# A sparse-attention and PReLU feed-forward kernel: batch 0 reordered over all engines, casts and copies in halves, layer 1 of chunk 0 woven into its end

## The chip, the cores and the metric

The kernel runs on 1 core of one Trainium2 chip. The metric is the device time of one execution in microseconds (us). The engines are TensorE (PE, with its weight loads shown as PEld), VectorE (DVE), ScalarE (ACT), GpSimd (POOL) and SyncE (SP, which here only issues DMAs). Each engine takes its own instructions in order and waits on semaphores for the others. Matmul results go to PSUM, everything else lives in SBUF.

## The reference

```python
q, k, v: (8, 8, 576, 64)            # batch, heads, positions, head size
scores = q @ k^T / 8
mask, heads 0-3: 0 <= i - j < 32                     # local
mask, heads 4-7: i >= j and i % 32 == j % 32         # strided
attn = softmax(masked scores) @ v
x = attn.transpose(0, 2, 1, 3).reshape(4608, 512)    # 8 * 576 tokens
h = x @ w_in                                         # 512 -> 2048
g = max(h, 0) + alpha * min(h, 0)
out = g @ w_out                                      # 2048 -> 512
```

Inputs and output are float32.

## The kernel before

**Units of work.** Attention is cut into 32 pairs of heads, four to a batch; pair g belongs to batch g // 4. Of the four pairs of a batch, 0 and 1 are local and 2 and 3 strided. The feed-forward part is cut into 9 chunks of 512 tokens. Layer 1 of a chunk is 16 blocks m of four 128x128 by 512 matmuls (`lin1_piece`, L652), each followed by ACT (`neg`, L662) and DVE (`gT`, L665). Layer 2 of chunks 0 and 1 is 16 pieces of four matmuls (`lin2_piece`, L679), four to one block of 128 output rows, which ACT copies out (L684) and SP stores (L685). From chunk 2 on layer 2 uses seven products of a Strassen-like scheme (`lin2_sums`, L771), with sums of weights in `wsum` and, in place in `wout16`, `w3` (`w_sums`, L711).

**Attention of a pair.** `transpose_piece` (T) turns q or k with eight PE transposes into a PSUM tile `tp`, which is copied to `qT` or `kT`; `tails` does the last 64 positions. For batches 0 and 1 the copy of `tp` is split by head `e`, one half on DVE and one on ACT (lines L190 and L188 of the helper `cast_copy`; L192 is its POOL form). `score_piece` (S) computes half of a pair's scores and, for batch 0, adds the mask by a matmul (L377) ahead of the exponential on ACT (L382, L385). `pv_piece` (P) multiplies by V with a column of ones and divides on DVE: a reciprocal (L478) and a product (L480). `x_piece` (X) transposes the result back, and a copy puts it into `xT`, layer 1's input. Batches 0 and 1 take this way (`NEARLY = 2`); from batch 2 on the strided q and k are turned by DMA transposes on SP (`transpose_d`, L137) and the masks are multiplied on POOL (L436, L443).

**PSUM.** Eight banks: a pool of three for `tp`, `tt`, `pv` and `xp` (tag "ps"), two for `sp`, and three (`banks`, picked in turn by `hbank`) for layers 1 and 2. In batch 0 two of these three serve scores and the third takes filler matmuls on zeros (`warm`, L829).

**Loads.** POOL issues nearly all of them, in this order at the start: tails, q and k of the local heads, V, the four quarters of `w_in` (`win`), of `w_out` (`wout`), then all of batch 1. Between the issues POOL does casts: local q and k (`cast_l`), half of V (`cast_v`), and `over_v`, which copies a part of the local V tile to other partitions. SP issues the strided k, the constants and later the stores and DMA transposes.

**Order.** The function `alone` writes out the order of batches 0 and 1 by hand into the list `pieces`. All of batch 0 runs before any layer 1:

```python
fns = [T(u0, "q"), T(u0, "k"), Sc(A[0], 0), Sc(A[0], 1), T(u1, "q"), Sc(A[1], 0), T(u1, "k")]
fns += [Sc(A[1], 1), Sc(L[0], 0), Pv(A[0], 0), Sc(L[0], 1), Pv(A[0], 1), Pv(A[0], 2)]
```

Here u0 is the strided unit, u1 the local one, A and L their pairs. Then layer 1 of chunk 0 runs alone, 16 blocks; then layer 2 of chunk 0, with the 22 pieces of batch 1 spread between its 16 pieces by a list of counts, and after them the two transposes of batch 2's local heads. From chunk 1 on, attention of batch n + 1 is spread evenly between the blocks of chunk n. Chunk 1's layer 1 needs batch 1, as 448 of its tokens lie in it.

Of the kernel before, what the change touches and what calls it, by code (L numbers as in the profile page):

```python
# [31 lines left out]
def kernel(  # L32
# [112 lines left out]
                cast_copy(eng[f], t16[:, f : f + 1, :], loaded[(b, True, nm)][:, f : f + 1, :])  # L145
        cast16[(b, True, nm)] = t16

    def cast_l(b, nm, eng="pool"):
        t16 = hpool.tile([128, 8, 2, 64], F16, tag=f"{nm}l16", bufs=2, name=f"{nm}l16")
        cast_copy(eng, t16, loaded[(b, False, nm)].rearrange("p f (t d) -> p t f d", t=8))  # L150
        cast16[(b, False, nm)] = t16

    def load_tail(b, strided):

# [44 lines left out]
                      "p (h t d) -> p h t d", h=2, t=8))  # L199
        cast16[(b, True, "v")] = v16  # L200

    def over_v(b, eng):

        v16 = vls[b % 2]
        cast_copy(eng, v16[0:32, 1:24, :], v16[96:128, 0:23, :])


    class Pair:
# [25 lines left out]
    def transpose_piece(u, nm):  # L234

        b, strided = u // 2, u % 2 == 1  # L240
        early = b < NEARLY
        src = cast16[(b, strided, nm)]
        dst = qTs[u % 2][:, :, 0:576] if nm == "q" else kTs[u % 2][:, :, 32:608]
        if early and nm == "k":
            tails(b, u, strided)
        tp = pspool.tile([128, 8, 64, 2], F16, tag="ps", name="tp")
        for j in range(8):
            blk = (src[:, j % 2, 128 * (j // 2) : 128 * (j // 2) + 128] if strided
                   else src[:, j].rearrange("p f d -> p (f d)"))
            keep(nc.tensor.transpose(tp[:, j].rearrange("r p e -> r (p e)"), blk, ident))  # L250
        if strided:
            main = tp.rearrange("r j p e -> r e j p")
            o = dst.rearrange("r e (j p) -> r e j p", j=8)[:, :, :, 0:64]
        else:
            main = tp.rearrange("r t p e -> r e p t")
            o = dst[:, :, 0:512].rearrange("r e (p t) -> r e p t", t=8)
        if early:
            for e in range(2):
                eng = "dve" if (nm == "q") == (e == 0) else "act"
                if u == 0 and nm == "q":  # L260
                    eng = "dve"
                cast_copy(eng, o[:, e : e + 1], main[:, e : e + 1])
            return
        cast_copy("act", o, main)
        if nm == "k":
            tails(b, u, strided)

    def tails(b, u, strided):
# [216 lines left out]
    def x_piece(P):  # L485
        xp = pspool.tile([128, 1024], F16, tag="ps", name="xp")
        for t in range(P.n):
            keep(nc.tensor.transpose(  # L488
                xp[:, P.w * t : P.w * t + P.w], P.x16[0 : P.w, 128 * t : 128 * t + 128], ident[0 : P.w, 0 : P.w]))
        base = (P.b % 4) * S  # L490
        if P.strided:
            keep(nc.scalar.copy(
                xT[:, P.hp, base : base + S].rearrange("r (p t) -> r p t", t=8),
                xp[:, 0:576].rearrange("r (t p) -> r p t", t=8)))
        else:
            cast_copy("act" if P.b < NEARLY and P.hp == 0 else "dve",
                      xT[:, P.hp, base : base + S], xp[:, 0:576])

    def x_dma(P):
# [21 lines left out]
    def T(u, nm):  # L521
        return lambda: transpose_piece(u, nm)
# [10 lines left out]
    def alone(u0, u1):  # L533

        A, L = (2 * u0, 2 * u0 + 1), (2 * u1, 2 * u1 + 1)

        def Sb(g):
            return lambda: score_early(pairs[g])

        if u0 == 1:  # L540
            fns = [T(u0, "q"), T(u0, "k"), Sc(A[0], 0), Sc(A[0], 1), T(u1, "q"), Sc(A[1], 0), T(u1, "k")]
            fns += [Sc(A[1], 1), Sc(L[0], 0), Pv(A[0], 0), Sc(L[0], 1), Pv(A[0], 1), Pv(A[0], 2)]
            fns += [Sc(L[1], 0), Pv(A[1], 0), Sc(L[1], 1), Pv(A[1], 1), Pv(A[1], 2)]
        else:
            fns = [T(u0, "q"), T(u0, "k"), Sb(A[0]), Sb(A[1])]
            fns += [Pv(A[0], 0), T(u1, "q"), Pv(A[0], 1), T(u1, "k"), Pv(A[0], 2), Sb(L[0])]
            fns += [Pv(A[1], 0), Pv(A[1], 1), Sb(L[1]), Pv(A[1], 2)]
        fns += [Pv(L[0], 0), X(A[0]), Pv(L[0], 1), X(A[1])]
        fns += [Pv(L[1], 0), Pv(L[1], 1), X(L[0]), X(L[1])]
        for fn in fns:  # L550
            feed(fn, -1)

    alone(1, 0)
    end0 = len(pieces)
    alone(3, 2)
    end1 = len(pieces)

# [81 lines left out]

    gTs = {}  # L640

    def lin1_piece(n, m):
        if m == 0:
            gTs[n] = gpool.tile([128, 16, 512], F16, tag="gT", name="gT")
        c0 = (512 * n) % RING
        parts = [(c0, 0, min(512, RING - c0))]
        if c0 + 512 > RING:
            parts.append((0, RING - c0, 512 - (RING - c0)))
        hps = hbank()
        for kk in range(4):  # L650
            for x, (src, dst, w) in enumerate(parts):
                keep(nc.tensor.matmul(  # L652
                    hps[:, dst : dst + w],
                    win16[:, kk, 128 * m : 128 * m + 128],
                    xT[:, kk, src : src + w],
                    start=(kk == 0 and x == 0),
                    stop=(kk == 3 and x == len(parts) - 1),
                    skip_group_check=True,
                ))

        neg = npool.tile([128, 512], F32, tag="neg", name="neg")
        keep(nc.scalar.activation(neg, hps, AF.Relu, scale=-1.0))  # L662

        def fin():
            keep(nc.vector.scalar_tensor_tensor(  # L665
                gTs[n][:, m, :], neg, oma[:, m : m + 1], hps, op0=ALU.mult, op1=ALU.add))
        late.append(fin)
# [28 lines left out]

        return wout16[:, 8 * i : 8 * i + 8, 256 * j : 256 * j + 256]

    def w_sums(eng, which):

        w1, w2, w4 = wsum
        w3 = wq(0, 1)
        steps = {
            1: (w1, wq(0, 1), wq(0, 0), ALU.subtract),
            2: (w2, wq(1, 1), w1, ALU.subtract),
            3: (w3, wq(1, 1), wq(0, 1), ALU.subtract),
            4: (w4, wq(1, 0), w2, ALU.subtract),
        }
        for z in which:
            o, x, y, op = steps[z]  # L710
            keep(eng.tensor_tensor(o, x, y, op=op))  # L711

    def g_sum(eng, n, which, k0, k1):

# [153 lines left out]
    load_v(0, True)  # L868
    load_v(0, False)
    load_w(0, False)  # L870
    cast_l(0, "q")
    load_w(1, False)
    cast_l(0, "k")
    load_w(2, False)
    load_w(3, False)
    cast_v(0, 1, "pool")
    over_v(0, "pool")
    for c in range(4):
        load_w(c, True)
    load_unit(1, True)  # L880
    load_unit(1, False)

    warm(12)
    keep(nc.vector.tensor_copy(id16, ident[0:16, 0:16]))
    cast_s(0, "q", ("dve", "act"))
    cast_s(0, "k", ("dve", "act"))
    keep(nc.vector.tensor_scalar(
        madd, consts[:, 128:488], -1.0, 30000.0, op0=ALU.add, op1=ALU.mult))
    apt = pspool.tile([128, 512], F32, tag="ps", name="apt")
    for i in range(end0):  # L890
        if i == 3:
            keep(nc.tensor.transpose(apt[:, 0:16], alpha_r, id16))
            keep(nc.vector.tensor_scalar(
                oma, apt[:, 0:16], -1.0, 1.0, op0=ALU.mult, op1=ALU.add))
        if i == 8:
            cast_v(0, 0, "dve")
        attn_step(end0)
        if i < 2:
            warm(4 - i)
        elif i > 8 and i not in (10, 13, 15):  # L900
            warm(1)

    def attn_n(n, end):
        for _ in range(n):
# [16 lines left out]
    cast_l(2, "k")  # L921


    turn.append(2)
    for m in range(16):
        lin1_piece(0, m)
        attn_n(0, end1)
    for i in range(16):
        lin2_piece(0, i)
        attn_n((0, 1, 1, 1, 1, 2, 1, 2, 1, 2, 1, 2, 2, 3, 2, 0)[i], end1)  # L930
        if i > 13:
            attn_n(1, end1 + 2)
    assert pos["i"] == end1 + 2
    wide["on"] = False
    load_unit(3, False)
# [2 lines left out]
    for n in range(1, NCH):  # L938
        ab = attn_until(n + 1) if n + 1 < B else len(pieces)
        left = ab - pos["i"]  # L940
        acc = 0.0
        for i in range(32 if n == 1 else 30):
            second["on"] = i >= 16
            if i < 16:
                if n > 1:
                    lin1_piece(n, {13: 7, 14: 14}.get(i, 8 * (i % 2) + i // 2))
                    if i in (5, 9, 13):
                        g_sum(nc.gpsimd, n, 1, i // 2 - 2, i // 2)
                else:
                    lin1_piece(n, i)  # L950
            elif n == 1:
                lin2_piece(n, i - 16)
                if i in (18, 22, 26):
                    w_sums(nc.vector, ({18: 1, 22: 2, 26: 4}[i],))
            else:
                lin2_sums(n, i - 16)
                if n == 2 and i == 20:
                    w_sums(nc.vector, (3,))
            if n < B - 2 or i < 16 or i > 19:
                acc += left / (22.5 if n == 1 else 16 if n == B - 2 else 20.5) * (0.5 if i < 16 else 1.0)  # L960
            cnt = int(acc)
            acc -= cnt
            attn_n(cnt, ab)
        while pos["i"] < ab:
            attn_step(ab)
# [30 lines left out]
```

The softmax here doesn't subtract the row's maximum and nothing guards it: scores larger than these inputs give would overflow.

## Time and profile before

| What | Value |
|---|---|
| median of 6 runs | 305.31 us (305.21 to 305.67) |
| the profiled execution, its own time | 305.27 us |
| its span (first to last instruction) | 303.5 us |
| PE busy | 294.7 us, 97% of the span |
| DVE, ACT, POOL busy | 221.2, 177.6, 171.5 us |
| DMA moved | 40.38 MB, mean 133 GB/s |
| end of attention of batch 0 (last `xT` copy) | 24.33 us |
| first matmul of chunk 0's layer 2 | 37.97 us |
| first matmul of chunk 1's layer 1 | 60.88 us |

A row of the timeline has the start in us, the duration in us, engine, line, operation, out<-in, shapes and a count; in brackets stands the idle time of that engine before it and what ended it. A row of the waits has who waited for whom, the sum in us, how often, and the longest. "PE busy" counts filler matmuls too, and the modelled end of a matmul lies some 0.17 us after its last column. A DMA share above 1 means that more than one packet was under way on an engine on average.

### The profile page before, as it was taken

What the parts mean: (1) busy time and instruction counts of PE and PEld (TensorE: products, weight loads), DVE (VectorE), ACT (ScalarE), POOL (GpSimd) and SP (SyncE); (2) the same over time, 40 slices, a digit from 0 to 9 for tenths busy, and PEclk for the clock granted to TensorE, in tenths of its full rate; (3) what the DMA queues carried; (4) which work ended last, traced back from release to release, by engine and by line L of the source; (5) the groups of instructions that cost most, each with busy time, mean ns of one, the idle gap of its engine ahead of it and who ended that gap; (6) DMA issues with size and microseconds to landing.
All of it is one profiled execution on the core that took longest, in us unless ns stands there. A gap on an engine that the chain in (4) does not pass through costs nothing.

```text
span 303.5 us, 7042 instructions
## 1 busy us (share of the span) xinstructions
PE 294.7 (97%) x2786; PEld 191.3 (63%) x2786; DVE 221.2 (73%) x417; ACT 177.6 (59%) x330; POOL 171.5 (57%) x176
## 2 busy tenths in 40 slices
PE   7799999999999999999999999999999999999995
PEld 2454455644555468746888887458845874684484
DVE  5686856758783889488848884888578958845872
ACT  3655754697547774677567755766477246516620
POOL 8872369946999864877397729771746003101300
PEclk9999999999999999999999999999999999999999
DMA  7999998999699992999399919971921070012004
GB/s 224 198 206 206 204 225 213 170 164 246 183 163 195 208 107 40 161 282 119 47 168 275 115 28 162 171 91 30 185 68 23 0 162 0 2 69 72 0 0 140
DMA packets 81201, 40.38 MB, mean 133 GB/s; under 512 B 58624, under 2 KB 76304, under 8 KB 81168
## 3 DMA queue, kind: packets, MB, share of 16 engines
q0 software_dynamic: 41728, 17.38, 48.2%
q1 hardware_dynamic: 39168, 22.03, 32.8%
q10 hardware_dynamic: 272, 0.52, 0.6%
q8 instruction: 22, 0.36, 0.5%
q14 instruction: 11, 0.09, 0.1%
HBM read 38.01 MB, written 9.44 MB: 156 GB/s over the span
## 4 chain that ended last, share of the span: by engine, by line
PE 88%; DVE 5%; ACT 2%; DMA 2%; issue 1%; SPq 0%; ACTq 0%
PE hb L652 41%; PE hb L771 25%; PE hb L679 9%; PE pv L469 4%; PE tp L250 2%; DMA kl<-in_k_dram 2%; PE sp L421 2%; PE xp L488 1%; PE opl L771 1%; DVE gsum L723 1%; DVE qT L190 1%; PE sph L421 1%; ACT kT L188 1%; PE hb L829 1%; DVE x L480 1%
## 5 line engine op out<-in xcount | busy, mean ns | idle before, releaser
L652 PE MATMUL hb<-xT,win 128*128 128x512 f16 (+1 forms) x640 | 132.0, 358 | 0.1
L665 DVE SCALAR_TENSOR_TENSOR gT<-neg,oma,hb 128x512 f16<-128x512 f32 x144 | 105.4, 744 | 36.2 <-ACT neg L662 28.3
L662 ACT ACTIVATE neg<-hb 128x512 f32<-128x512 f32 x144 | 86.1, 598 | 36.4 <-PE hb L652 35.8
L652 PEld LDWEIGHTS <-win 128*128 128x128 f16 x640 | 60.0, 98 | 54.7 <-issue 0.4
L436 POOL TENSOR_TENSOR et<-et,consts 128x576 f16<-128x576 f16 (+1 forms) x24 | 30.7, 1278 | 40.7 <-ACT et L434 40.6
L723 POOL TENSOR_TENSOR gsum<-gT 128x512 f16<-128x512 f16 x21 | 24.2, 1151 | 52.0 <-DVE gT L665 52.0
L771 PEld LDWEIGHTS <-gsum 128*128 128x128 f16 x448 | 41.6, 98 | 4.9 <-DVE gsum L723 0.2
L480 DVE TENSOR_TENSOR x<-pv,rc 96x384 f16<-96x384 f32 (+2 forms) x62 | 33.0, 532 | 2.1
L771 PEld LDWEIGHTS <-gT 128*128 128x128 f16 x336 | 31.5, 98 | 4.8
L443 POOL TENSOR_TENSOR et<-et,consts 128x576 f16<-128x576 f16 (+1 forms) x24 | 32.8, 1366 | 2.2 <-ACT et L440 2.2
L679 PE MATMUL hb<-wout,gT 128*128 128x512 f16 x128 | 32.3, 379 | 0.1
L469 PEld LDWEIGHTS <-et 72*128 72x128 f16 (+1 forms) x448 | 23.6, 98 | 10.7 <-issue 1.3
L783 ACT COPY o<-hb 128x512 f32<-128x512 f32 (+1 forms) x28 | 15.8, 565 | 24.1 <-PE hb L771 24.1
L771 PE MATMUL hb<-wout,gT 128*128 128x256 f16 x216 | 27.3, 273 | 0.0
L771 PE MATMUL hb<-wout,gsum 128*128 128x256 f16 x216 | 26.9, 273 | 0.0
L434 ACT ACTIVATE et<-sp 128x576 f16<-128x576 f32 (+1 forms) x24 | 15.5, 645 | 18.3 <-PE sp L421 18.3
L771 PE MATMUL hb<-wsum,gsum 128*128 128x256 f16 x216 | 26.0, 273 | 0.0
L786 DVE TENSOR_TENSOR o<-hb,o 128x512 f32<-128x512 f32 (+1 forms) x21 | 14.3, 679 | 14.7 <-PE hb L771 10.9
L478 DVE RECIPROCAL rc<-pv 72x6 f32<-72x6 f32 (+2 forms) x80 | 14.6, 183 | 10.7 <-PE pv L469 10.5
L440 ACT ACTIVATE et<-sph 128x288 f16<-128x288 f32 (+1 forms) x48 | 18.9, 409 | 0.0
L679 PEld LDWEIGHTS <-gT 128*128 128x128 f16 x128 | 10.7, 97 | 9.1
L469 PE MATMUL pv<-vs,et 72*128 72x65 f16 x256 | 15.5, 193 | 0.7 <-DVE vs L190 0.4
(103 smaller groups left out, 321.1 us busy)
## 6 DMA issues: line engine op xcount, KB each, us to landing
out_dram<-o SPq DMA_DIRECT2D x27, 256.0 KB, 3.6
kl<-in_k_dram SPq DMA_DIRECT2D x6, 512.0 KB, 7.7
ql<-in_q_dram SPq DMA_DIRECT2D x5, 512.0 KB, 7.3
stv<-in_v_dram POOLq DMA_DIRECT2D x8, 288.0 KB, 7.3
vl<-in_v_dram POOLq DMA_DIRECT2D x6, 384.0 KB, 10.0
win<-in_moe_w_in_dram POOLq DMA_DIRECT2D x4, 512.0 KB, 10.7
wout<-in_moe_w_out_dram POOLq DMA_DIRECT2D x4, 512.0 KB, 13.7
out_dram<-osb SPq DMA_DIRECT2D x8, 256.0 KB, 5.5
```

Of the source, the lines that this page charges most:

```text
L436: keep(nc.gpsimd.tensor_tensor(mv, mv, m, op=ALU.mult))
L440: keep(nc.scalar.activation(ev[:, n * y : n * y + n], sps[y][0:r, 0:n], AF.Exp, scale=SCALE))
L443: keep(nc.gpsimd.tensor_tensor(mv, mv, m, op=ALU.mult))
L469: keep(nc.tensor.matmul(pv[:, 65 * x : 65 * x + 65], et[0:r, c : c + 128], v16[0:r, 2 * P.pr + hh, t, :] if P.strided else v16[:, 6 * (2 * ...
L480: keep(nc.vector.tensor_tensor(P.x16[0:w, c0 : c0 + 64 * nb].rearrange("r (c e) -> r c e", e=64), pvv[:, :, 0:64], rc[0:w, 0:nb].unsqueeze ...
L652: keep(nc.tensor.matmul(hps[:, dst : dst + w], win16[:, kk, 128 * m : 128 * m + 128], xT[:, kk, src : src + w], start=(kk == 0 and x == 0) ...
L662: keep(nc.scalar.activation(neg, hps, AF.Relu, scale=-1.0))
L665: keep(nc.vector.scalar_tensor_tensor(gTs[n][:, m, :], neg, oma[:, m : m + 1], hps, op0=ALU.mult, op1=ALU.add))
L679: keep(nc.tensor.matmul(ops, gTs[n][:, kf, 128 * mt : 128 * mt + 128], wout16[:, kf, :], start=(kf == 0), stop=(kf == 15)))
L723: keep(eng.tensor_tensor(o[:, k0:k1], x[:, k0:k1], y[:, k0:k1], op=op))
L771: keep(nc.tensor.matmul(dst, lhs[:, kf, 128 * mt : 128 * mt + 128], rhs[:, kf, :], start=(first and own and kf == 0), stop=(kf == 7), skip ...
L783: keep(nc.scalar.copy(o, x))
```

## The change

1. Batch 0 leaves the list `pieces` and gets an order of its own, written out over all engines as a list of small steps: transposes, tails, scores, outputs, casts, V copies and loads.
2. `transpose_piece` for batches 0 and 1 makes two PSUM tiles of four transposes each; one tile is copied by DVE, the other by ACT (for the strided q of batch 0 both by ACT). Before it was one tile of eight, split by head. `tails` of batch 0 become steps of their own.
3. The casts of batch 0's local q and k go half to POOL, half to DVE; `over_v` is done in two halves; two loads of `wout` are issued ahead of it. The loads of batch 1 are issued after the list.
4. Nine of the twelve matmuls of layer 1's blocks m = 2, 1, 0 of chunk 0 (inputs of heads 2 to 7) run among the last outputs of batch 0. The remaining one of each and then blocks 3 to 15 follow. `xT` of pair 0 of batch 0 is copied by DVE, before by ACT.
5. In layer 2 of chunk 0 the attention pieces of batch 1 start after the fourth piece and come closer together towards the end. Batch 1 uses one order with `score_early`, as before.
6. `w3` is formed in three parts in the last pieces of chunk 1's layer 2, before in one part in chunk 2.

```diff
-        tp = pspool.tile([128, 8, 64, 2], F16, tag="ps", name="tp")
-        for j in range(8):
...
-        if early:
-            for e in range(2):
-                eng = "dve" if (nm == "q") == (e == 0) else "act"
-                if u == 0 and nm == "q":
-                    eng = "dve"
-                cast_copy(eng, o[:, e : e + 1], main[:, e : e + 1])
-            return
+        halves = 2 if early else 1
+        nj = 8 // halves
+        for z in range(halves):
+            tp = pspool.tile([128, nj, 64, 2], F16, tag="ps", name="tp")
+            for x in range(nj):
+                j = nj * z + x
...
+            eng = "act"
+            if early and ((nm == "q") == (z == 0)) and (u, nm) != (1, "q"):
+                eng = "dve"
+            cast_copy(eng, o, main)
...
-            cast_copy("act" if P.b < NEARLY and P.hp == 0 else "dve",
+            cast_copy("act" if P.b == 1 and P.hp == 0 else "dve",
...
+    def lin1_mm(n, m, kks, first, last):
+        if first:
+            hcur[m] = hbank()
+        hps = hcur[m]
...
+    def lin1_piece(n, m):
+        if n not in gTs:
+            gTs[n] = gpool.tile([128, 16, 512], F16, tag="gT", name="gT")
+        if n == 0 and m < 3:
+            hps = lin1_mm(n, m, (0,), False, True)
+        else:
+            hps = lin1_mm(n, m, range(4), True, True)
...
+    first = [
+        ("C", "q", 0, "pool"), ("D", (1, False)),
+        ("T", 1, "q"), ("W", 2), ("t", 1), ("W", 1), ("A",), ("C", "q", 1, "dve"), ("C", "k", 0, "pool"),
+        ("D", (2, False), (3, False)), ("V", 1, "pool"), ("D", (0, True), (1, True)),
+        ("W", 1), ("T", 1, "k"), ("T", 0, "q"), ("W", 1), ("C", "k", 1, "dve"),
+        ("S", 2, 0), ("t", 0), ("S", 2, 1), ("T", 0, "k"), ("S", 3, 0), ("W", 1), ("V", 0, "dve"),
+        ("S", 3, 1), ("O", 12, 24), ("P", 2, 0), ("P", 2, 1), ("W", 1), ("P", 3, 0), ("S", 0, 0),
+        ("O", 1, 12), ("P", 2, 2), ("S", 1, 0), ("P", 3, 1), ("S", 1, 1), ("W", 2), ("P", 3, 2),
+        ("X", 2), ("P", 1, 0), ("S", 0, 1), ("P", 0, 0), ("X", 3), ("W", 1), ("P", 1, 1), ("B",),
+        ("L", 2, 2), ("L", 1, 2), ("P", 0, 1), ("L", 0, 2), ("L", 1, 3), ("X", 1), ("L", 2, 3),
+        ("X", 0), ("L", 0, 3), ("L", 2, 1), ("L", 1, 1), ("L", 0, 1),
+    ]
+    for z in first:
+        do[z[0]](*z[1:])
+    w_next((2, True), (3, True))
+    load_unit(1, True)
+    load_unit(1, False)
...
-    for m in range(16):
+    for m in (2, 1, 0, *range(3, 16)):
         lin1_piece(0, m)
...
-        attn_n((0, 1, 1, 1, 1, 2, 1, 2, 1, 2, 1, 2, 2, 3, 2, 0)[i], end1)
-        if i > 13:
-            attn_n(1, end1 + 2)
+        attn_n((0, 0, 0, 1, 0, 1, 1, 1, 2, 2, 2, 2, 3, 3, 2, 2)[i], end1)
+        if i == 15:
+            attn_n(2, end1 + 2)
...
+                if i > 28:
+                    k0, k1 = {29: (0, 2), 30: (2, 4), 31: (4, 8)}[i]
+                    w_sums(nc.vector, (3,), k0, k1)
...
-                if n == 2 and i == 20:
-                    w_sums(nc.vector, (3,))
```

In the list T, t, S, P and X are the pieces named above (with unit or pair and part), C a half cast of local q or k, V a half of the V copy, O a part of `over_v`, D loads of `win` (False) or `wout` (True), A the slope `oma` = 1 - alpha, W filler matmuls, L one matmul of layer 1 (block m, input pair), and B gives the third bank to layer 1.

## The prediction

> **What bounds the kernel now.** I read the page's busy shares and slices first, then the sums of four stretches, then the timeline of the first stretch, then each place later on where TensorE (PE) waits.
>
> ```profile
> PE 294.7 (97%) x2786; PEld 191.3 (63%) x2786; DVE 221.2 (73%) x417; ACT 177.6 (59%) x330; POOL 171.5 (57%) x176
> ```
>
> PE is the bound nearly everywhere; an edit pays only where PE waits or does filler. Sums by stretch (PE busy, then PEld, DVE, ACT, POOL, clock, DMA share, GB/s), cut at the first full layer-1 stream, the first layer-2 matmul, the first matmul of chunk 1, and the first strided score of batch 2:
>
> ```profile
> 0.00:24.38 24.38, 20.06 (x230) 11.12 (x231) 16.16 (x49) 11.80 (x24) 19.08 (x33) 1.00 1.26 209
> 24.38:37.97 13.59, 13.59 (x63) 6.13 (x63) 10.49 (x15) 8.96 (x15) 3.82 (x6) 1.00 1.26 205
> 37.97:60.88 22.91, 22.27 (x262) 13.10 (x261) 15.20 (x38) 12.90 (x28) 19.89 (x22) 1.00 1.45 203
> 60.88:72.65 11.77, 11.77 (x87) 5.39 (x86) 8.48 (x15) 9.89 (x20) 7.75 (x7) 1.00 1.56 160
> ```
>
> The loss is in the first 24 us, whose PE "busy" also hides warm-up filler. DMA is loaded in all four stretches (share over 1), which matters below. Inside the first stretch:
>
> ```profile
> 14.99 0.42 DVE L190 COPY vs<-stv 72x1024 f16<-72x1024 f16 x1
> 15.85 0.19 DVE L478 RECIPROCAL rc<-pv 72x6 f32<-72x6 f32 x1 [0.43 <-PE pv L469]
> ...
> 22.92 0.55 DVE L480 TENSOR_TENSOR x<-pv,rc 96x384 f16<-96x384 f32 x1
> 23.87 0.46 DVE L190 COPY xT<-xp 128x576 f16<-128x576 f16 x1 [0.40 <-PE xp L488]
> ```
>
> Ten attention outputs (reciprocal plus product) leave through DVE one after another from 15.85 to 23.47, and they start only when DVE has made the V copy at 14.99. The waits of 5 to 25 us show why that is late:
>
> ```profile
> DVE kT L190 <- ACT kT L188: 1.9, 2, 1.1
> ACT qT L188 <- DVE qT L190: 1.3, 1, 1.3
> ```
>
> Two halves of one transpose tile are copied out by DVE and ACT, and one waits for the other. Later PE waits in one place that the change touches, in the chunk-2 stretch: DVE forms `w3` at 116.65 and only then an attention output that PE needs:
>
> ```profile
> 116.58 1.22 DVE L711 TENSOR_TENSOR wout<-wout 128x2048 f16<-128x2048 f16 x1
> 118.39 0.36 PE L469 MATMUL pv<-vs,et 72*128 72x65 f16 x6 [0.31 <-DVE x16s L480]
> ```
>
> [...] the trace has equal DVE casts of 0.43 us (`qs`) and 1.09 us (`ks`, while POOL was issuing), which bound the moved casts. [...] the store issued at 55.14 behind POOL's loads took 7.0 us to land.
>
> **Part 1, batch 0.** Halves by blocks put each half in its own bank, so no copy waits for its twin. I rolled the new orders forward with durations of before: ACT half copy 0.59, DVE 0.69, exponentials 0.65 and 2 x 0.35, POOL cast of half 0.52 (half of 1.03), landings as before. DVE: `ks` cast to 8.10, `madd` and tails to 8.6, slope 8.8, half of `ql` (landed 8.84) to 9.3, kT 10.0, local qT 10.7, half of `kl` (landed 10.59) to 11.2, local kT 12.4 to 13.1, V copy 13.1 to 13.5. Four transposes instead of eight before a copy, and the locals' transposes ahead of the first score, fill the old holes; the first score stays at 10.25 (10.26 before). First attention output: 13.55 instead of 15.46. Then DVE has ten outputs, eight of 0.70 and two of 0.62 from start to start, 6.85 us: 13.95 to 20.8 (before 7.6, as it waited for PE three times). Two xT copies of 0.46 end at 21.8 (24.33 before). By then 9 of layer 1's 64 matmuls have run in the holes (9 x 0.218 = 2.0; 0.218 is the chain's 13.76 over 63).
>
> A new wait: three banks end together, so block m=3 needs bank 2 back: its last matmul ends at 22.4, ACT 0.60, DVE 0.74, so 23.8, while PE is through at 22.6: 1.2 us lost. Then 52 x 0.218 = 11.3: layer 2 starts at 35.2 instead of 37.97, **2.8 us earlier**. If the DVE casts take 1.09 instead of 0.43, 0.7 to 1.3 later; without the bank wait, 1.2 earlier. Queues passed: POOL issues two `wout` loads ahead of the overlap copy of V, and the loads of batch 1 follow the list. The order of bytes is the same and the DMA engines are full, so landings stay: the last `win` at 25.3 (needed about 31), the last `wout` at 36.0 (needed 37.8). Moving one xT copy to DVE (0.46) is in the sum. The second instruction of the halved POOL copy costs nothing while POOL waits 1.8 us for `vl` there; uncovered, some 0.1 (estimate).
>
> **Part 2, batch 1 under layer 2.** Same PE work, 22.9 us before, of which I count 2.1 as gaps (from matmul start to start[...]). Batch 1's data do not move: POOL's cast of `kl` was held by its landing (45.08) and ended at 46.2. With attention pushed behind block 4, that transpose comes 11.2 us after layer 2's start, at 46.4, so it just fits; the first store, now about 4 us earlier among these loads, may delay `kl` by the 0.7 us that 256 KB take at 385 GB/s, the best that the DMA view shows; one psum slot wait (0.5) and one wait for the last output (0.4) replace the old gaps. I take 22.4 to 23.0: chunk 1 starts at 57.6 to 58.2, **2.7 to 3.3 us earlier**. POOL runs without a pause from 45.13 to 56.8, when batch 2's `kl` cast ends; that just precedes its transpose.
>
> **Part 3, what is late next.** From here PE's order is unchanged, and PE would run 3 us ahead of data that do not move. Two floors:
>
> ```profile
> 61.75 2.63 SPq L137 DMA_TRANSPOSE qT<-qsd  x1
> ...
> 64.49 4.13 SPq L137 DMA_TRANSPOSE kT<-ksd  x1
> ...
> 66.12 2.01 POOL L192 COPY vs<-stv 72x1024 f16<-72x1024 f16 x2
> ...
> 68.08 0.82 POOL L172 DMA_DIRECT2D stv<-in_v_dram  x1
> ...
> 68.92 1.30 POOL L443 TENSOR_TENSOR et<-et,consts 128x576 f16<-128x576 f16 x1
> ```
>
> First, `stv` lands at 64.0 (issue 53.21 plus 10.8). Behind it on POOL stand two copies, an issue and the mask that the second local attention piece (PE, 70.63) needs: 4.2 us, so 68.2 at best, and later if the transposes cut in. Second, `kT` lands at 72.1 (64.49 plus 7.6) and the strided score runs at 72.65. In the new order the fourth store leaves at about 57 instead of 61.23, so SP can issue `qT` when `qsd` has landed, 60.2 rather than 61.75; but POOL's backlog is the same and the 16 engines are full, so the bytes before `kT` are conserved. It may land as before (gain of PE there 0.5) or up to 2.5 earlier. I take 71.3, gain **1.3 us** (0.6 to 2.2).
>
> **Part 4, w3.** The 1.14 us leave chunk 2; PE waited 0.31 there (0.47 from start to start): gain **0.4** (0 to 0.5). It comes back as three pieces in chunk 1's last blocks, where DVE stood idle 1.74 us before 92.72 and 2.71 before 96.21: nothing; uncovered, 1.2.
>
> **Sum.** 1.3 + 0.4 = 1.7 us off the profiled execution's 305.27 (span 303.5 plus 1.77 around it), which is 0.04 below the median 305.31: **303.6**.
>
> **Rivals.**
> Carried through (0.25): the 16 engines had room and the floors move with PE. For it: share above 1 counts overlap, not bytes, and the rate in 60 to 72 is only 140 to 180 GB/s. Against: the fourth store waited 3 us behind POOL's loads. 3.0 + 0.4: about 301.9 (301.2 to 302.6).
> Absorbed (0.14): `kT` lands where it did[...] and the head start is lost: 0 to 0.6, so 304.7 to 305.9.
> Slower (0.11): the earlier stores push `kl`, and with it POOL's serial chain and `qsd`, by two stores (1.4 us). `kT` then lands at 73.5 and PE waits 0.9 more than before; with part 4 worth 0.4 to 0 that is 305.8 to 306.2, 306.0 in the middle. It decides once `kT` lands after 73.0, which uses up both the 0.5 of slack and the 0.4.
> Capped, as forecast: 0.50, 302.8 to 304.6.
>
> **The numbers.** 0.2% is 0.6 us, about what a measurement of this kernel tells from no change. Faster: 0.25 + 0.50 + a little of the absorbed case, 0.78. Same 0.13, slower 0.09. The range, 301.3 to 305.3, leaves out the slower case and the ends of two others.
>
> **What would show it.** First attention output near 13.6; last xT copy near 21.8; a bank wait of about 1 us at m=3; layer 2 at 35; chunk 1 at 58; then PE waiting for POOL's mask near 69 or for `kT` near 71. Wrong if no such wait appears (then 302), if layer 2 starts after 37, or if `kT` lands after 73.

## The result and the profile after

The changed kernel took **308.05 us** in the median (306.18 to 312.53, 35 runs) against 305.36 (304.92 to 309.47, 72 runs) for the kernel before: a ratio of **1.0077** (95% interval 1.0065 to 1.0089), slower. 303.6 had been predicted, with 305.3 as the upper end. The ratio leaves the most disturbed runs out. The profiled execution took 306.43 us (span 304.6), 1.16 more than that of before.

| Milestone, us | before | predicted | after | after minus before |
|---|---|---|---|---|
| first attention output on PE | 15.46 | 13.55 | 14.15 | -1.31 |
| first matmul of layer 2, chunk 0 | 37.97 | 35.2 | 35.63 | -2.34 |
| first matmul of chunk 1 | 60.88 | 57.6 to 58.2 | 60.07 | -0.81 |
| first strided score of batch 2 | 72.65 | 71.3 or so | 71.84 | -0.81 |
| first matmul of chunk 2 | 94.51 | | 93.71 | -0.80 |
| first matmul of chunk 2's layer 2 | 110.03 | | 111.56 | +1.53 |
| end of the span | 303.49 | 301.8 | 304.57 | +1.08 |

The head start of 2.34 us shrinks to 0.8 under batch 1; within chunk 2 it turns into a loss of 1.5; then 0.47 comes back. The sums of the same four stretches as before, first the line of engine totals (columns: the stretch, its length, busy time and instructions of PE, PEld, DVE, ACT and POOL, clock, DMA share, GB/s):

```profile
PE 293.0 (96%) x2775; PEld 191.0 (63%) x2775; DVE 226.9 (75%) x420; ACT 177.5 (58%) x331; POOL 171.5 (56%) x177
```

```profile
0.00:24.41 24.41, 20.19 (x230) 11.48 (x230) 17.58 (x52) 13.53 (x28) 18.38 (x34) 1.00 1.26 211
24.41:35.63 11.22, 11.22 (x53) 5.08 (x52) 9.52 (x14) 7.32 (x13) 2.73 (x4) 1.00 1.24 204
35.63:60.07 24.44, 22.74 (x262) 13.35 (x260) 15.68 (x38) 12.49 (x28) 21.02 (x23) 1.00 1.39 211
60.07:71.84 11.77, 11.77 (x87) 5.37 (x85) 8.39 (x15) 10.05 (x20) 8.09 (x8) 1.00 1.95 193
```

The second row has 53 matmuls of layer 1 where there were 63: part 1 works. The third is 1.5 us longer than before, with PE standing 1.7 of it. The first sign of the loss is in the first line: PE is busy 1.7 us less and DVE 5.7 us more, though the change gives DVE only small copies and casts. The timeline of DVE late in chunk 1 shows where most of the 5.7 us are:

```profile
91.92 0.19 DVE L481 RECIPROCAL rc<-pv 96x6 f32<-96x6 f32 x1 [0.83 <-PE pv L472]
92.14 0.55 DVE L483 TENSOR_TENSOR x<-pv,rc 96x384 f16<-96x384 f32 x1
92.62 5.50 DVE L718 TENSOR_TENSOR wout<-wout 128x512 f16<-128x512 f16 x2
98.04 2.05 DVE L672 SCALAR_TENSOR_TENSOR gT<-neg,oma,hb 128x512 f16<-128x512 f32 x3
```

The row of 5.50 is the second and third part of `w3`; the second alone runs from 92.62 to 97.52. A whole sum takes 1.2 us elsewhere, so a quarter is 0.3 and the half after it 0.6. The same time on POOL:

```profile
91.93 0.81 POOL L175 DMA_DIRECT2D stv<-in_v_dram  x1
92.75 1.29 POOL L439 TENSOR_TENSOR et<-et,consts 128x576 f16<-128x576 f16 x1
94.00 1.28 POOL L446 TENSOR_TENSOR et<-et,consts 128x576 f16<-128x576 f16 x1
95.22 1.03 POOL L195 CAST ql<-ql 128x1024 f16<-128x1024 f32 x1
96.20 1.03 POOL L195 CAST kl<-kl 128x1024 f16<-128x1024 f32 x1
97.19 1.50 POOL L183 DMA_DIRECT2D vl<-in_v_dram  x1
```

Two masks and two casts follow each other without a hole, each at its usual length, and the second part of the sum ends 0.33 us after POOL turns to issuing a DMA. Its row begins at 92.62, 0.13 ahead of the first mask, and lasts 4.90 us, through all four instructions and the three boundaries between them; the third part then takes 0.68. What holds the sum back isn't shown. Behind the sum stands `gT`, and PE stands for it (to the matmul rate, 2.35 us):

```profile
98.83 1.89 PE L650 MATMUL hb<-xT,win 128*128 128x512 f16 x8 [2.18 <-DVE gT L672]
```

So the profiled executions balance: -0.81 from the start, +2.35 here, -0.47 for the wait near 118 that is gone, together +1.07, and the spans differ by 1.08.

The median differs by more, 2.69. Of the 36 executions, the profiled one among them, 18 have a mean granted clock of 0.998 to 1.0 and a median of 306.96 (+1.6); 15 have 0.992 to 0.994 (median 308.64) and 3 have 0.989 (312.1). For the 72 runs of the kernel before the clock is not on record. Of the 161 that were taken beside the experiments, 156 have 0.998 or more and five have 0.989 to 0.994, three of these with no longer time (305.19 to 305.57). The second experiment shows where in an execution the lower clock stands.

### The profile page after: what moved, and what is told of

Read it like the earlier page. It is cut to its first block, busy times and chain, and to the rows that moved or that the text cites. A ratio compares the mean times of both kernels' runs of the same rounds, so it can differ in the third digit from the quotient of the medians.

```text
span 304.6 us, 7025 instructions
## 1 busy us (share of the span) xinstructions
PE 293.0 (96%) x2775; PEld 191.0 (63%) x2775; DVE 226.9 (75%) x420; ACT 177.5 (58%) x331; POOL 171.5 (56%) x177
## 4 chain that ended last, share of the span: by engine, by line
PE 89%; DVE 6%; DMA 2%; ACT 1%; POOL 1%; issue 1%; POOLq 0%
PE hb L650 40%; PE hb L778 27%; PE hb L686 8%; PE pv L472 4%; PE tp L257 3%; DMA ql<-in_q_dram 2%; PE sp L424 2%; DVE x L483 2%; DVE wout L718 2%; PE opl L778 1%; PE xp L491 1%; PE sph L424 1%; DVE rc L481 1%; DVE gT L672 0%; POOL tl L161 0%
## 5 line engine op out<-in xcount | busy, mean ns | idle before, releaser
L195 POOL COPY vs<-stv 72x1024 f16<-72x1024 f16 x15 | 15.4, 1047 | 0.4 <-DMA stv<-in_v_dram 0.4
```

## The experiments

Three theories stood at the start. **A**: `w3` in its new place is held back by POOL's work. **C**: the new list of batch 1 costs what batch 0's order gains. **D**: the halves of batch 1's transposes (two PSUM tiles for one) make the crowding. Each expectation states its own case.

**e1, the changed kernel with `w3` in its old place.**

```diff
-                if i > 28:
-                    k0, k1 = {29: (0, 2), 30: (2, 4), 31: (4, 8)}[i]
-                    w_sums(nc.vector, (3,), k0, k1)
...
+                if n == 2 and i == 20:
+                    w_sums(nc.vector, (3,))
```

> The changed kernel with part 6 alone undone (w3 again in one piece in chunk 2). Theory A, w3 moved among POOL's work is the loss (its last two parts took 5.5 us on DVE, PE stood 2.35 us at 98.8): 306.4, the profiled execution, minus 2.35 plus the 0.3 that PE waits in chunk 2 again: about 304.4, below the kernel before. Theory B, the DVE block there is only where a lateness shows that comes from elsewhere: a wait of about 2 us appears elsewhere and the time stays at 306.4. On the scatter (306.2 to 312.5, TensorE clock 1.000 to 0.989 over an execution): if PE's pause at 98.8 brings the lower clock, scatter and low clock go; if the start with fewer filler matmuls brings it, they stay and the median lies 1 to 2 us above the fastest.

Measured: 305.99 (304.07 to 311.26), ratio 1.001 (0.9992 to 1.0029). Two of the lost 2.7 us come back, and the fastest run gains 2.1, but the median misses the 304.4 expected, as the runs scatter over 7 us. Its profiled execution (307.44) shows one reason: now another sum, `w4` in `wsum`, is caught in the same way. DVE, then POOL:

```profile
86.93 0.55 DVE L483 TENSOR_TENSOR x<-pv,rc 72x384 f16<-72x384 f32 x1
87.40 5.26 DVE L718 TENSOR_TENSOR wsum<-wout,wsum 128x2048 f16<-128x2048 f16 x1
```

```profile
87.11 1.30 POOL L439 TENSOR_TENSOR et<-et,consts 128x576 f16<-128x576 f16 x1
88.34 1.28 POOL L446 TENSOR_TENSOR et<-et,consts 128x576 f16<-128x576 f16 x1
89.56 2.02 POOL L195 COPY vs<-stv 72x1024 f16<-72x1024 f16 x2
91.52 0.81 POOL L175 DMA_DIRECT2D stv<-in_v_dram  x1
```

The sum ends 1.14 us after POOL turned to issuing a DMA, about one whole sum (1.21), as the quarter above ended 0.33 after (0.3 by itself): both look like a sum that waits for the end of the chain and then runs at its usual speed. PE then waits 2.87 us at 93.41. In the profiled execution of the changed kernel the same sum started at 87.34, 0.24 us ahead of the second mask, took 1.36, and the mask beside it 2.25 in place of 1.28. So either engine can win: between the two executions the sum's start differs by 0.06 us and that of POOL's first mask by 0.77 (86.34 and 87.11). The wider form of theory A is that all sums of weights which stand among POOL's work are such a lottery.

**e2, the kernel before with `w3` in three parts (part 6 of the change alone).** The edit is that of e1 the other way round, on the kernel before.

> The kernel before with part 6 alone (w3 in three parts at the end of chunk 1). Theory A: PE waits about 2.3 us near 98 to 100 and 0.4 less in chunk 2, so 305.3 + 2.0 = 307.3. Theory B: no such wait in this kernel, 305.0. If the pause of PE brings the lower clock, the clock falls below 1.000 in some executions here too.

Measured: 308.82 (307.19 to 309.92, 6 runs), ratio 1.0101 (1.008 to 1.0121). This part alone costs 3.5 us, more than the whole change does; the one of its six runs at full clock took 307.19, near the 307.3 expected. The sum is blocked as in the changed kernel, and its profiled execution shows what follows when PE has stood. DVE and PE:

```profile
93.42 5.49 DVE L711 TENSOR_TENSOR wout<-wout 128x512 f16<-128x512 f16 x2
98.84 1.39 DVE L665 SCALAR_TENSOR_TENSOR gT<-neg,oma,hb 128x512 f16<-128x512 f32 x2
```

```profile
99.62 3.54 PE L652 MATMUL hb<-xT,win 128*128 128x512 f16 x8 [2.18 <-DVE gT L665]
```

The same eight matmuls took 1.89 us in the changed kernel's profiled execution and take 3.54 here: the trace has the granted clock at 0.5 for 3.4 us, from 99.6 to 103.0, beginning just as PE resumes (columns as in the stretches above):

```profile
99.60:103.00 3.40, 3.38 (x8) 1.01 (x7) 2.69 (x5) 0.60 (x1) 0.00 (x0) 0.50 1.81 194
```

That costs 1.7 us, half of 3.4, and spread over 305 us it is the mean clock of 0.992 to 0.994 that 15 of the changed kernel's runs show (by the same estimate 0.989 would be two such stretches); the medians of these 15 and of the 18 at full clock differ by 1.7 too. So a pause of 2.3 us can cost 4.0. It doesn't always: the changed kernel's own profiled execution stood 2.35 us, and the 3.47 us behind that, 98.83 to 102.30, have the clock at 1.00. Nor is it the longer pauses that the lower clock follows. In the rows of PE the idle time is 2.18 us in e2 and 2.33 in e8 below, whose executions have mean clocks of 0.994; it is 2.18 in the changed kernel, 2.38 in e10 and 2.71 in e1, whose executions have 1.000. What decides isn't shown.

**e3, the kernel before with the new list for batch 1 (part 5 alone).**

```diff
-        attn_n((0, 1, 1, 1, 1, 2, 1, 2, 1, 2, 1, 2, 2, 3, 2, 0)[i], end1)
-        if i > 13:
-            attn_n(1, end1 + 2)
+        attn_n((0, 0, 0, 1, 0, 1, 1, 1, 2, 2, 2, 2, 3, 3, 2, 2)[i], end1)
+        if i == 15:
+            attn_n(2, end1 + 2)
```

> The kernel before with part 5 alone (batch 1's pieces start after the fourth piece of layer 2 and stand closer together at the end). In the changed kernel the stretch from layer 2 to chunk 1 took 24.4 us against 22.9. Theory C, the list does it: about 1 us slower, 306.3, with waits of PE at the outputs' and transposes' psum tiles. Theory D, the halved transposes do it (two psum tiles each where three are to be had): no change, 305.3.

Measured: 307.12 (306.99 to 307.86, 5 runs), ratio 1.0053 (1.0041 to 1.0065): **1.8 us slower**, and the layer-2 stretch takes 25.08 in place of 22.91:

```profile
37.88:62.96 25.08, 22.63 (x261) 13.33 (x260) 14.92 (x38) 12.68 (x28) 19.04 (x22) 1.00 1.44 199
```

Theory C holds for the kernel before: the denser list by itself costs some 2 us.

**e5, the changed kernel with the old list and `w3` back (batch 0's order and the halves alone).** The edit is e1's, and e3's the other way round.

> The changed kernel with parts 5 and 6 undone: what is left is batch 0's new order with the halves. If the list costs here what it cost alone (1.7 us), the fastest executions lie near 304.1 - 1.5 = 302.6. Rival, which would justify the list: layer 2 now starts at 35.7, before batch 1's data (q of the strided heads lands at 38.0), so the old list waits about 1 us for DMA and the gain is 0.5 or none: 303.6 to 304.1. The scatter of e1 (304.1 to 311.3) stays in both.

Measured: 305.35 (304.5 to 306.5), ratio 0.9993 (0.9976 to 1.0009), no difference, with the fastest run above both ranges expected. Layer 2 starts at 35.78, 2.2 us early, and chunk 1 at 61.06, 0.2 late. The stretch has no crowd at its end, but PE now runs into batch 1 before its data and DVE are ready:

```profile
39.69 0.27 PE L276 MATMUL tt<-consts,tl 64*128 64x64 f16 x4 [0.71 <-DMA tl<-in_k_dram]
41.64 0.30 PE L311 MATMUL sp<-qT,kT 64*128 64x72 f16 x8 [0.26 <-ACT kT L191]
46.79 0.36 PE L472 MATMUL pv<-vs,et 72*128 72x65 f16 x6 [0.77 <-DVE x L483]
48.82 0.40 PE L257 MATMUL tp<-consts,kl 128*128 128x128 f16 x4 [0.31 <-DVE x L483]
```

So both lists lose the head start: the old one early, by data and DVE; the new one late, by crowding. The list was put off for a reason, and its price is 0.8 us less than that of leaving it (60.07 to 61.06, less the 0.15 between the two starts). The scatter did not stay as expected: the 14 runs lie within 2.0 us at full clock, though the sums stand where e1 has them. So a shift in time alone may take a kernel out of the scatter, and little scatter does not prove that the sums stand well.

**e4, e1 with batch 1's transposes whole and split by head, as before.**

```diff
-        halves = 2 if early else 1
+        halves = 2 if b == 0 else 1
...
+            if b == 1:
+                for e in range(2):
+                    eng = "dve" if (nm == "q") == (e == 0) else "act"
+                    cast_copy(eng, o[:, e : e + 1], main[:, e : e + 1])
+                continue
```

> As e1_w3_back, and batch 1's transposes again in one psum tile of eight, split by head as in the kernel before; batch 0 stays in halves. Theory D: the waits at 48.5 and 49.2 (0.76 and 0.48) shrink to some 0.5 in all and chunk 1 starts 0.7 earlier: 303.7 where e1 gives 304.4. Theory C: as e1, within 0.2.

Measured: 305.64 (304.33 to 314.32), ratio 1.0009 (0.9989 to 1.0029). The stretch takes 24.57 (35.30 to 59.87) and has one wait of 1.38 us at 48.80 in place of the two of 0.76 and 0.48. Theory D falls: the wait for the copies is the same in both shapes.

**e6, e1 with the other sums where POOL has no such chain ("calm").** `w1` and `w2` are formed at the start of chunk 1, when POOL rests (60.0 to 63.7), `w4` after the third piece of its layer 2.

```diff
+        if n == 1:
+            w_sums(nc.vector, (1, 2))
...
-                if i in (18, 22, 26):
-                    w_sums(nc.vector, ({18: 1, 22: 2, 26: 4}[i],))
+                if i == 18:
+                    w_sums(nc.vector, (4,))
```

> e1_w3_back with two more sums moved away from POOL's work: w1 and w2 (1.2 us each) are formed at the start of chunk 1, where POOL stands idle some 3 us, and w4 where w1 was. Theory A in its wider form ([...] 5.3 us for w4 in e1's profile, 1.35 in before's): scatter goes, all executions within 1 us, median at e1's fastest, 304.1 to 304.6, TensorE clock 1.000. Rival (the scatter comes from DMA or from the start): median stays near 306 and 2 to 5 us of scatter stay.

Measured: **305.08** (304.55 to 306.45, 22 runs), ratio **0.9984** (0.9973 to 0.9994): no run above 306.5, no lowered clock in any of the 22, and a little faster than the kernel before. Every sum takes 1.21 to 1.64 us in its profiled execution. The median misses the 304.1 to 304.6 expected and the spread is 1.9 us where 1 was. The fall of the scatter fits the wider theory A; e5 above and e7, e8 and e10 below show that the places of the sums are not all of it. The new place isn't free: `gT` comes late once, PE waits 0.58 us at 63.21, and the old wait of 0.47 near 118 is back with `w3`.

**e11, the kernel before with the same calm places.** The edit is e6's.

> The kernel before with w1 and w2 formed at the start of chunk 1 and w4 after the third piece of its layer 2, nothing else changed. If the gain of 0.3 of the calm version of the changed kernel came from the places of the sums alone (batch 0's new order worth nothing at the end), this gives the same: 305.0 to 305.1. If the sums cost the kernel before nothing where they stood (its wait there was under 0.3), it stays at 305.3 to 305.5, or 305.8 if the two sums in a row delay gT by the 0.58 seen in the calm version, and the gain is batch 0's.

Measured: 306.03 (305.38 to 308.63), ratio 1.0021 (1.0006 to 1.0035): slower, the third of the cases expected. DVE and PE:

```profile
61.89 1.22 DVE L711 TENSOR_TENSOR wsum<-wout 128x2048 f16<-128x2048 f16 x1
63.14 1.22 DVE L711 TENSOR_TENSOR wsum<-wout,wsum 128x2048 f16<-128x2048 f16 x1
64.28 2.06 DVE L665 SCALAR_TENSOR_TENSOR gT<-neg,oma,hb 128x512 f16<-128x512 f32 x3
```

```profile
65.07 1.24 PE L652 MATMUL hb<-xT,win 128*128 128x512 f16 x5 [0.41 <-DVE gT L665]
```

So e6's gain doesn't come from the places. With the same places, parts 1 to 5 of the change are worth about **1 us** (306.03 - 305.08 = 0.95; against the runs of the kernel before in each one's own set, +0.71 and -0.37, so 1.1). The 0.81 of the milestones is of that size.

**e7 and e8, e6 with other lists.** e7 has the old list; e8 one between the two:

```diff
-        attn_n((0, 0, 0, 1, 0, 1, 1, 1, 2, 2, 2, 2, 3, 3, 2, 2)[i], end1)
+        attn_n((0, 0, 1, 1, 1, 1, 2, 1, 2, 1, 2, 2, 2, 2, 3, 1)[i], end1)
```

> e6_calm with the old list of batch 1. With the wide theory A and the list's 1.7: 302.6 to 303.2, little scatter. If the old list waits for DMA: as e6.

> e6_calm with a list between the two: the old one begun one piece later, 0 0 1 1 1 1 2 1 2 1 2 2 2 2 3 1. If both costs are real (crowding and data): the best of the three, about 302.6; otherwise between e6 and e7.

Measured: e7 305.83 (305.47 to 312.47), ratio 1.0005 (0.9986 to 1.0025), stretch 25.09: 0.75 above e6, neither of its cases, and 2 of its 14 runs have a clock of 0.989 and 0.994 although the sums are calm. e8 305.58 (304.61 to 310.65), ratio 1.0011 (0.999 to 1.0031). e8 lies between e6 and e7, its second case. It has the shortest stretch of all with an early start, 23.73, and chunk 1 at 59.11, and gains nothing by it: its 16 runs at full clock have a median of 305.06. In its profiled execution (307.84) PE then stands for a DMA transpose, issued at 61.85:

```profile
73.75 0.42 PE L424 MATMUL sp<-qT,kT 64*128 64x72 f16 x8 [2.33 <-DMA kT<-ksd]
...
74.34 3.15 PE L650 MATMUL hb<-xT,win 128*128 128x512 f16 x8
```

and then runs slowly again (eight matmuls in 3.15 us in place of 1.89; mean clock of this execution 0.994). The floor of part 3 of the prediction is there, 2.5 us deep in this execution.

**e9, the changed kernel with `w3` whole in chunk 2, where POOL rests.**

```diff
-                if i > 28:
-                    k0, k1 = {29: (0, 2), 30: (2, 4), 31: (4, 8)}[i]
-                    w_sums(nc.vector, (3,), k0, k1)
...
                     lin1_piece(n, {13: 7, 14: 14}.get(i, 8 * (i % 2) + i // 2))
+                    if n == 2 and i == 4:
+                        w_sums(nc.vector, (3,))
```

> The changed kernel, but w3 is formed in one piece in chunk 2, after its fifth layer-1 block, a place where POOL has an idle stretch of about 1.6 us. Theory [...]: the sum takes 1.2 to 1.7 us, no wait of over 1 us stands before the end of chunk 1's layer 2 because of it, and the 0.47 us wait near 118 stays away: fastest run 304.0 to 304.6 in place of 306.2, w1, w2 and w4 still scatter the median up to 306. Theory 'it is the three parts' own work on DVE, wherever it stands': a PE wait of 1 us or more appears in chunk 2's first blocks and the fastest run is at 305.5 or above.

Measured: 305.93 (304.32 to 311.7), ratio 1.0006 (0.9983 to 1.0028). As theory A had it for `w3`: 2.1 us less than the changed kernel in the median, the fastest run within its forecast. DVE, POOL and PE in its profiled execution (304.43):

```profile
98.92 1.22 DVE L718 TENSOR_TENSOR wout<-wout 128x2048 f16<-128x2048 f16 x1
```

```profile
99.34 1.93 POOL L439 TENSOR_TENSOR et<-et,consts 72x576 f16<-72x576 f16 x1 [1.14 <-ACT et L437]
```

```profile
100.84 1.02 PE L650 MATMUL hb<-xT,win 128*128 128x512 f16 x4 [0.56 <-DVE gT L672]
```

Here DVE came first, and it is POOL's mask that is stretched, from 1.27 to 1.93: the same meeting from the other side. The whole sum costs PE 0.72 us once (that wait, to the matmul rate) and saves 0.47 near 118. The scatter stays; `w1`, `w2` and `w4` stand where they were.

**e10, all four sums at places where POOL rests**: e9 with `w1` ahead of chunk 1, `w2` after its 13th block, `w4` after the 8th piece of its layer 2.

```diff
+        if n == 1:
+            w_sums(nc.vector, (1,))
...
                     lin1_piece(n, i)
+                    if i == 12:
+                        w_sums(nc.vector, (2,))
...
-                if i in (18, 22, 26):
-                    w_sums(nc.vector, ({18: 1, 22: 2, 26: 4}[i],))
+                if i == 23:
+                    w_sums(nc.vector, (4,))
```

> The changed kernel with every weight sum put where POOL rests: w1 before chunk 1's first block, w2 after its 13th block, w4 after the 8th piece of its layer 2, w3 after the 5th block of chunk 2. [...] every sum takes 1.2 to 1.7 us, none of the waits of 0.58 at 63, 2.2 at 99 and 0.47 at 118 is there, no scatter: against the kernel with w1, w2 and w4 calm and w3 in its old place (305.08) about 0.9 less, 304.2 (303.9 to 304.7). If what remains is something else (DMA landings, crowding), it stays at 304.9 to 305.3.

Measured: 305.83 (304.59 to 309.06), ratio 1.003 (1.001 to 1.0049), a little slower than the kernel before: **the expectation failed**. Every sum does take 1.21 us (1.22 at most), and none of the waits behind the sums is left but 0.72 at 103.9; yet it isn't faster, and it scatters. In its profiled execution (307.48) PE waits elsewhere:

```profile
74.62 0.30 PE L424 MATMUL sp<-qT,kT 64*128 64x72 f16 x8 [2.38 <-DMA kT<-ksd]
```

So a sum behind POOL's chain lengthens some executions (e1), and a late `kT` others (e8, e10). Times of the two DMA transposes in the thirteen profiled executions, in order of the issue of `qT`:

| Kernel | `qT` issued | `kT` issued | `kT` landed | strided score | wait for `kT` |
|---|---|---|---|---|---|
| e8 | 59.02 | 61.85 | 73.70 | 73.75 | 2.5 |
| e9 | 59.17 | 61.22 | 70.23 | 71.55 | |
| e4 | 59.26 | 61.30 | 70.25 | 71.64 | |
| after | 59.46 | 61.37 | 70.65 | 71.84 | |
| e1 | 59.63 | 61.64 | 71.53 | 71.90 | |
| e10 | 59.80 | 62.09 | 74.58 | 74.62 | 2.5 |
| e6 | 60.49 | 62.60 | 71.02 | 71.92 | |
| e7 | 61.64 | 63.60 | 71.14 | 73.01 | |
| e2 | 61.74 | 63.98 | 70.9 | 72.64 | |
| before | 61.75 | 64.49 | 72.11 | 72.65 | |
| e5 | 61.93 | 63.74 | 71.25 | 72.83 | |
| e3 | 62.35 | 65.29 | 70.3 | 74.73 | |
| e11 | 62.42 | 64.21 | 71.56 | 73.78 | |

Issuing up to 3 us earlier never brought `kT` before 70.2; from issue to landing it takes 5.0 to 7.6 us in the last six rows and 8.9 to 12.5 in the first six. e3 issued `kT` last of all and had it 1.8 us before the kernel before. In eleven of the thirteen the landing lies within 70.2 to 72.1, for issues from 61.2 to 65.3, so the issue isn't what sets it. Where the strided score runs at 71.6 to 71.9, the margin is 0.4 to 1.4 us, so a landing after 72 is a wait. What sends it to 74 in some executions isn't shown.

## Why the prediction was wrong, point by point

- **Part 1, batch 0: the mechanism right, the size 0.4 off.** Layer 2 started 2.34 us earlier, for 2.8. The two copies of the local `kT` ran side by side (0.69 us on DVE from 12.57, 0.58 on ACT from 12.60); in the kernel before, those of the strided one came one after the other (ACT from 9.59, DVE from 10.24). The new wait for the third bank came where it was named and with its size: 1.20 at 24.41 (1.2 predicted), the last `xT` copy at 22.36 (21.8). The first output came 0.6 later than worked out, and the mis-sized term is the V copy on DVE: 0.91 us, where I used the 0.42 of before. It ran beside POOL's half of the V copy (12.77 to 13.81) and ended 0.28 after that; in the kernel before POOL's half was over when DVE's began. A delay beside POOL's work I had allowed for the casts (0.7 to 1.3 later) and not for this copy; no run tests it here alone.

```profile
12.57 0.69 DVE L193 COPY kT<-tp 128x512 f16<-128x512 f16 x1 [0.81 <-PE tp L257]
13.18 0.91 DVE L193 COPY vs<-stv 72x1024 f16<-72x1024 f16 x1
```

- **Part 2, batch 1 under layer 2: wrong by 1.4 to 2.0 us.** I took 22.4 to 23.0 us, it took 24.44. The 2.1 of old gaps was an estimate of mine. I allowed 0.5 for one wait for a PSUM slot and 0.4 for one for the last output; the trace of the changed kernel has five waits, together 2.5 to the matmul rate, four of which the PE timeline names (the fifth is 0.30 at 58.82):

```profile
45.10 1.02 PE L686 MATMUL hb<-wout,gT 128*128 128x512 f16 x4 [0.19 <-ACT osb L691]
48.52 0.38 PE L257 MATMUL tp<-consts,kl 128*128 128x128 f16 x4 [0.60 <-DVE qT L193]
49.21 0.40 PE L257 MATMUL tp<-consts,kl 128*128 128x128 f16 x4 [0.31 <-DVE x L483]
55.78 0.42 PE L491 MATMUL xp<-consts,x 72*128 72x72 f16 x8 [0.47 <-ACT xT L495]
```

  None waits for data: `kl` landed at 43.43 and not at 45.08 or later, so the fear that stood behind my slower rival points the wrong way. The waits are for DVE and ACT to empty PSUM, which fits 22 pieces standing where there is room for fewer. e3 prices this in the kernel before at 1.8 us, e4 excludes the halves, and e5 shows that the old list would have lost as much to data.
- **Part 3, the floors: right as a mechanism, not what set this result.** I put `kT` at 71.3 and it landed at 70.65; PE reached the strided score at 71.84 with no wait, as its head start was only 0.81. That the DMA engines were full, so that landings stay, was not shown: at 193 to 211 GB/s in the four stretches (160 to 209 before), `kl` landed 1.65 and `kT` 1.46 us earlier than before. The bound of "up to 2.5 earlier" was not met either; e8 and e10 show that when PE is early the floor can be at 73.7 or 74.6, later than in the kernel before. "Carried through" (0.25) was therefore not to be had.
- **Part 4, w3: the failing step.** The gain in chunk 2 came as said (0.47; I took 0.4). The price of the new place was the step "where DVE stood idle 1.74 us ... and 2.71 ...: nothing; uncovered, 1.2". It cost 2.35 us in the profiled execution and some 4 where the half clock followed. I had seen a DVE cast take 1.09 us in place of 0.43 while POOL was issuing, used it to bound the casts in part 1, and did not ask of this place what POOL does there. The trace of the kernel before has both, the chain at that very place and a sum, `w2`, that takes 2.14 us in place of 1.21 beside a mask:

```profile
83.99 1.28 POOL L443 TENSOR_TENSOR et<-et,consts 72x576 f16<-72x576 f16 x1
84.22 2.14 DVE L711 TENSOR_TENSOR wsum<-wout,wsum 128x2048 f16<-128x2048 f16 x1
...
93.37 1.30 POOL L436 TENSOR_TENSOR et<-et,consts 128x576 f16<-128x576 f16 x1
94.61 1.29 POOL L443 TENSOR_TENSOR et<-et,consts 128x576 f16<-128x576 f16 x1
95.83 1.05 POOL L192 CAST ql<-ql 128x1024 f16<-128x1024 f32 x1
96.81 1.04 POOL L192 CAST kl<-kl 128x1024 f16<-128x1024 f32 x1
```

  DVE's idle time was no cover, because POOL's chain of four instructions (4.5 us) ran all through it, and so "the work of a sum" (1.2) was no upper bound either: what it cost here was the rest of POOL's chain. e1, e2 and e9 show it from three sides: 5.26 us for a whole sum beside such a chain, 5.49 for the last two parts of `w3`, and 1.22 for the whole of it in e9's place. Taking this step back is not enough to reach the forecast: e1's median is 305.99 and its fastest run 304.07.
- **The rivals.** The one on the other side (306.0, by `kT` after 73.0) named a mechanism that e8 and e10 show, but it was not that of this kernel. The one that happened, a sum held back behind POOL's chain, was not among them.
- **The sum.** Predicted: 1.3 + 0.4 earlier. Measured in the profiled execution: 0.81 + 0.47 earlier and 2.35 later. One small reading was off and changes nothing: the best that the DMA view shows is 398 GB/s, not 385.

Left open: what holds a DVE sum back beside POOL's chain, and what decides which of the two is stretched; what decides whether the half clock follows a pause of PE; what lengthens the runs of e7 and e9 that have no profile; and what makes `kT` land at 70 or 74. The version that the runs point to, e6 with `w3` in e9's place, has no measured time.

## What to carry to other kernels

Before a sum like `w3` or `w4` is moved to a place where DVE is idle, look at POOL's row for the same time: an unbroken chain there can hold the sum back to its end (4.90 us for 0.3 in the changed kernel, 5.26 for 1.21 in e1), and all that stands behind it on DVE. A head start is worth only what the next stage can take up: ask for each of its waits (data, PSUM slots, the engine that empties them) which one is next. And when one kernel's runs scatter more than the other's, look for a race between two engines, or between an engine and a load, before averaging over it.

## What the runs showed of the hardware

- A DVE sum of two weight tensors that takes 1.22 us where POOL rests (e6, at 60.02) took 5.26 us (e1), and a quarter of it 4.90 (after), beside back-to-back POOL instructions; it ended 1.14 and 0.33 us after POOL turned to issuing a DMA. Where it began 0.42 (e9) and 0.24 us (after) ahead of one of POOL's masks, it took 1.22 and 1.36, and the mask 1.93 and 2.25 in place of 1.27 and 1.28.
- A pause of PE in the middle of a kernel was followed in e2 (2.18 us idle) by 3.4 us at a granted clock of 0.50, worth 1.7 us, and in e8 (2.33) by eight matmuls in 3.15 us in place of 1.89, at a mean clock of 0.994 for the execution. After 2.18 us (after), 2.38 (e10) and 2.71 (e1) the mean clock of the execution was 1.000.
- DMA transposes issued up to 3.3 us earlier than in the kernel before (e9), among loads under way, landed at best 1.9 us earlier (e9) and at times 2.5 us later (e10): 7.6 us from issue to landing became 8.9 (e4) to 12.5 (e10). One issued 0.8 us later (e3) took 5.0 and landed 1.8 us earlier.
